# Interleaving the first block's work with the weight unpacking, and joining the attention's small products

## Chip, cores, metric

One core of a Trainium2 chip. The metric is the device time of one launch in microseconds (us): the median of three runs of the kernel before is 931.48 us (930.40 to 931.63).

## What is computed

Chunked attention (each of 36 chunks of 64 tokens attends to itself, per head), then two MLPs: a PReLU MLP of width 2048 and a bilinear MLP of width 1536. The model width is 512, there are 2304 tokens, and inputs and output are float32.

```python
scores = (1 / sqrt(64)) * q_c @ k_c.T          # per chunk of 64 tokens and head
attn = softmax(scores)                          # with 1e-9 added to the sum
x = (attn @ v_c)  -> (2304, 512)
h = x @ w_in;  g = max(h, 0) + alpha * min(h, 0);  x = g @ w_out
out = ((x @ w_a) * (x @ w_b)) @ w_o
```

## The kernel before

TensorE (PE) multiplies, VectorE (DVE) and ScalarE (ACT) do the elementwise work, and SyncE's queue (SP) issues all DMAs. The kernel works a float32 product out as three products of float32r parts: each operand is split into a rounded part hi (`to_hi`, L78, a copy on ACT) and the rest lo (`to_lo`, L81, a subtraction on DVE); `three` (L293) multiplies hi·hi, hi·lo and lo·hi.

The weights arrive as 64-bit values. A unit is a 128x512 tile of weights (`units`, L89); the first MLP has 32 of them, i0, i1, then i2, o0, i3, o1 and so on. `w_load` (L96) brings a unit of 512 KB into one of three staging buffers. `unpack_ops` (L107) makes float32 of it: on DVE two 16-bit operations (L122, L126) that write the two halves of wz, on ACT the widening (L125), on DVE the shift-and-or (L129). After that `split` makes hi and lo of the unit.

Tokens go in blocks of 512, 256, 512, 512 and 512, a group being 128 tokens. An opening, written out by hand as a list of steps (`order1`, L478), computes the attention of the first block's four groups and unpacks the first four units. Then the loop at L488 takes the blocks. For each of 16 slices j of the first MLP it runs `s1` (L307: 12 products to h), `prelu` (L310: neg and pos on ACT, pos on DVE, gh on ACT, gl on DVE) and, two iterations late, `s2` (L324: 12 products into four accumulator banks). In block 0 each iteration also splits the two units unpacked in the iteration before (L509), unpacks two more (L510) and starts two or three weight loads (L511), all ahead of `prelu` in program order. Engines run in program order, so this order is the order of the work on each engine.

The attention of the next block is laid between these as steps: `att_steps` (L398) lists them, and `advance` (L493) issues them spread evenly over two slots per iteration (in block 0 from slot 8 on). For one group these are: `att_T` (L204), eight 128x128 transposes of k and q and two copies on ACT; `att_S` (L216), 32 products of 64x64 into two banks; `att_M` (L230) on DVE: maximum and subtraction; `att_X` (L244), the exponential on ACT; `att_N` (L247), the sum and the division on DVE; `att_PT` (L256), four transposes of the probabilities and a copy (eT); `att_O` (L265), 32 products of 64x64 into two banks, whose hi and lo become the next block's x. A pool of four PSUM banks (`ps_p`, L66) is shared by h and all of the attention; it goes round in the order of the calls. The second MLP (L533) has no attention beside it, and the change does not touch it.

Of the kernel before, what the change touches and what calls it, by code (L numbers as in the profile page):

```python
# [8 lines left out]
F32 = mybir.dt.float32  # L9
# [9 lines left out]
def chunk_attention_prelu_mlp_bilinear_mlp(  # L19
# [55 lines left out]
    def wtile(name, dt=F32R):  # L75
        return wp.tile([P, DM], dt, tag="w", name=name)
# [7 lines left out]
    def split(*a):  # L84
        to_hi(*a)
        to_lo(*a)
# [17 lines left out]
                out=raw.rearrange("p (k f) -> p k f", k=KD), in_=src.rearrange("(k p) f -> p k f", p=P)  # L104
            )

    def unpack_ops(i):  # L107

        raw = raws.pop(i)
        hw = raw.rearrange("p (f t) -> p f t", t=2)[:, :, 1]
        if i < len(units) - 4:
            x = wtile("wx", I32)
        else:
            x = tp.tile([P, DM], I32, tag="t", name="wx")
        xs[i] = x
        z = wtile("wz", I32)
        z2 = z.bitcast(U16).rearrange("p (f t) -> p f t", t=2)  # L120
        h2 = raw.bitcast(U16).rearrange("p (f t) -> p f t", t=4)
        yield nc.vector.tensor_scalar(  # L122
            out=z2[:, :, 0], in0=h2[:, :, 1], scalar1=13, scalar2=None, op0=ALU.logical_shift_right
        )
        yield nc.scalar.activation(out=x.bitcast(F32), in_=hw.bitcast(F32), func=AF.Copy, scale=2.0 ** -112)  # L125
        yield nc.vector.tensor_scalar(  # L126
            out=z2[:, :, 1], in0=h2[:, :, 3], scalar1=1 << 15, scalar2=None, op0=ALU.bitwise_and
        )
        yield nc.vector.scalar_tensor_tensor(  # L129
            out=x, in0=x, scalar=3, in1=z, op0=ALU.logical_shift_left, op1=ALU.bitwise_or  # L130
        )

    def w_parts(i):
        m, j = units[i]
# [36 lines left out]
    def runs(t, n):  # L171
        done = 0
        while done < n:
# [2 lines left out]
            yield done, step, b, s  # L176
            done += step

    def load(nm, u):
        a = att[nm, u] = wtile(f"{nm}{u}", F32)  # L180
        for off, n, b, s in runs(u * P, P):
            nc.sync.dma_start(
                out=a[off:off + n].rearrange("p (h d) -> p h d", h=H),
                in_={"q": q, "k": k, "v": v}[nm][b, :, s:s + n, :].rearrange("h p d -> p h d"),
            )

    def load_qk(u):
        load("k", u)
        load("q", u)

    def load_v(u):
        load("v", u)
# [3 lines left out]
    def att_bank(u, nm):  # L196

        if u < sizes[0] // P:
            n_early[0] += 1
            if n_early[0] % 2:  # L200
                return acc_p.tile([P, DM], F32, tag="acc", name=nm)
        return bank(nm)

    def att_T(u, nms="kq"):  # L204
        for nm in nms:
            src = att.pop((nm, u))
            ps = att_bank(u, "psT")
            for g in range(KD):
                nc.tensor.transpose(ps[:, g * P:(g + 1) * P], src[:, g * P:(g + 1) * P], ident)  # L209
            t = att[nm + "T", u] = wtile(f"{nm}T{u}", F32)  # L210
            nc.scalar.activation(out=t, in_=ps, func=AF.Copy)  # L211

    def half(i):
        return slice(i * CH, (i + 1) * CH)

    def att_S(u):  # L216
        qT, kT = (att.pop((nm, u)).rearrange("p (g t) -> p g t", g=KD) for nm in ("qT", "kT"))
        pss = [att_bank(u, "psS") for _ in range(2)]
        for y in range(2):
            for c in range(2):  # L220
                for e in range(2):
                    for x in (e, 1 - e):
                        r, g, t = half(e), 2 * x + y, half(c)
                        nc.tensor.matmul(  # L224
                            out=pss[e][half(x), half(2 * y + c)], lhsT=qT[r, g, t], rhs=kT[r, g, t],
                            start=True, stop=True,
                        )
        att["s", u] = pss
# [33 lines left out]
        nc.scalar.activation(out=t, in_=ps, func=AF.Copy)  # L262
        att["eT", u] = t

    def att_O(u, xh, xl, col):  # L265
        eT, v_ = att.pop(("eT", u)), att.pop(("v", u))
        pss = [att_bank(u, "psO") for _ in range(2)]
        for g in range(KD):
            x, y = divmod(g, 2)
            for c in range(2):  # L270
                for e in (c, 1 - c):
                    nc.tensor.matmul(  # L272
                        out=pss[c][half(e), half(g)], lhsT=v_[half(c), half(2 * g + e)],
                        rhs=eT[half(c), half(4 * e + 2 * y + x)], start=True, stop=True,
                    )
        cols = [slice(col + c * CH, col + (c + 1) * CH) for c in range(2)]
        return [
            (xh[:, :, f], xl[:, :, f], ps[:, :KD * CH].rearrange("p (g i) -> p g i", g=KD))
            for f, ps in zip(cols, pss)
        ]  # L280

    def each(fn, parts):
        for part in parts:
            fn(*part)
# [22 lines left out]
    def s1(j, x, n):  # L307
        return proj(W["i", j], x, n)[:, :n]

    def prelu(j, h):  # L310
        n = h.shape[1]
        pos = tp.tile([P, NB], F32, tag="t", name="pos")[:, :n]
        neg = tp.tile([P, NB], F32, tag="t", name="neg")[:, :n]
        nc.scalar.activation(out=neg, in_=h, func=AF.Relu, scale=-1.0)  # L314
        nc.scalar.activation(out=pos, in_=h, func=AF.Relu)  # L315
        nc.vector.scalar_tensor_tensor(  # L316
            out=pos, in0=neg, scalar=nalpha_sb[:, j:j + 1], in1=pos, op0=ALU.mult, op1=ALU.add
        )
        gh = gp.tile([P, NB], F32R, tag="gh", name="gh")[:, :n]
        gl = gp.tile([P, NB], F32R, tag="gl", name="gl")[:, :n]  # L320
        split(gh, gl, pos)
        return gh, gl

    def s2(j, g, acc, n):  # L324
        wh, wl = W["o", j]
# [70 lines left out]
            pend.pop(0)()  # L396

    def att_steps(b, x):  # L398
        t0, n = blocks[b]
        steps = []  # L400

        def last(u):
            o = att_O(u, *x, u * P - t0)
            each(to_hi, o)
            each(to_lo, o)
            if u + 2 < NU:
                load_v(u + 2)

        def first(u):
            att_T(u)  # L410
            if u + 1 < NU:
                load_qk(u + 1)

        us = range(t0 // P, (t0 + n) // P)
        for w in range(len(us) + 2):
            T, A, Z = us[w:w + 1], us[max(w - 1, 0):w], us[max(w - 2, 0):max(w - 1, 0)]
            for u in T:
                steps.append(lambda u=u: first(u))
            for u in A:
                steps.append(lambda u=u: (att_X(u), weave(att_N(u))))  # L420
            for u in Z:
                steps.append(lambda u=u: att_PT(u))
            for u in T:
                steps.append(lambda u=u: (att_S(u), att_M(u)))
            for u in Z:
                steps.append(lambda u=u: last(u))
        return steps

    with tc.manual_schedule():
        n0 = sizes[0] // P  # L430
# [52 lines left out]
        for t in order1.split():  # L483
            early[t[0]](int(t[1:]))
        done["unpack"], done["split"] = 4, 3
        nc.scalar.mul(nalpha_sb, alpha_sb, -1.0)

        for b, (t0, n) in enumerate(blocks):  # L488
            nxt = xtiles("x")
            steps = att_steps(b + 1, nxt) if b + 1 < NBLK else []  # L490
            taken = [0]

            def advance(slot, first=8 if b == 0 else 0, last=2 * J1 - 3, steps=steps, taken=taken):  # L493
                want = -(-len(steps) * (slot + 1 - first) // (last + 1 - first))
                while taken[0] < min(want, len(steps)):
                    steps[taken[0]]()
                    taken[0] += 1

            for j in range(J1):
                if b == 0:  # L500
                    if j == 1:
                        load_qk(n0)
                    if j == 2:
                        load_v(n0)
                    if j == 3:
                        load_v(n0 + 1)
                h = h0[0][:, :n] if not (b or j) else s1(j, x, n)
                if b == 0:
                    w_split(min(2 * j + 4, NU1))  # L509
                    w_unpack(min(2 * j + 6, NU1))  # L510
                    w_dma(min(2 * j + 9, NU1))  # L511
                advance(2 * j)
                g = prelu(j, h)

                def second(b=b, j=j, g=g, n=n, nxt=nxt):
                    if j == 0:
                        acc[0] = new_acc()
                    s2(j, g, acc[0], n)
                    if j == J1 - 1:
                        end1(b, acc[0], n, nxt)  # L520

                pend.append(second)
                flush(2)
                advance(2 * j + 1)
                if b == NBLK - 1 and j >= 2:
                    ready = NU1 + 3 * (j - 2) // 2
                    w_dma(ready + 3)
                    w_unpack(ready + 1)
                    w_split(ready)
            x = nxt  # L530
# [60 lines left out]
```

## Time and profile before

| | |
|---|---|
| median of 3 runs | 931.48 us |
| profiled execution, its own time | 930.36 us |
| its span, first to last instruction | 928.6 us |
| PE busy | 904.1 us (97%) |
| DVE busy | 408.1 us (44%) |
| ACT busy | 337.1 us (36%) |
| DMA, mean over the span | 68 GB/s |

How to read it: a share is an average over stages. The opening lasts to some 31 us, block 0 to about 132, block 1 (256 tokens) to 193, blocks 2 and 3 to 389; then come the last block of the first MLP and the second MLP. In the timeline rows the columns are the start, the duration (a row of several instructions: from the first's start to the last's end), engine, line, operation, output and inputs, shape, count, and in brackets the idle time before and what ended it. Instructions on one engine overlap at their ends, so the pace of a stream is the distance between starts.

### The profile page before, as it was taken

What the parts mean: (1) busy time and instruction counts of PE and PEld (TensorE: products, weight loads), DVE (VectorE), ACT (ScalarE), POOL (GpSimd) and SP (SyncE); (2) the same over time, 40 slices, a digit from 0 to 9 for tenths busy, and PEclk for the clock granted to TensorE, in tenths of its full rate; (3) what the DMA queues carried; (4) which work ended last, traced back from release to release, by engine and by line L of the source; (5) the groups of instructions that cost most, each with busy time, mean ns of one, the idle gap of its engine ahead of it and who ended that gap; (6) DMA issues with size and microseconds to landing.
All of it is one profiled execution on the core that took longest, in us unless ns stands there. A gap on an engine that the chain in (4) does not pass through costs nothing.

```text
span 928.6 us, 13023 instructions
## 1 busy us (share of the span) xinstructions
PE 904.1 (97%) x5426; PEld 756.6 (81%) x5426; DVE 408.1 (44%) x762; ACT 337.1 (36%) x636; POOL 0.7 (0%) x6
## 2 busy tenths in 40 slices
PE   7889799999999999999999999999999999999998
PEld 5667689988888887888888888888888888888897
DVE  5888865543433443358865662211221122111212
ACT  5655655443343443345644442111121112111211
POOL 0000000000000000000000000000000000000000
PEclk9999999999999999999999999999999999999999
DMA  8665423221111300044433430200020002000100
GB/s 207 210 204 174 147 58 103 58 55 37 38 33 23 91 13 12 1 159 137 156 116 91 137 114 1 90 1 1 1 91 0 1 1 69 1 0 1 46 1 23
DMA packets 88810, 62.70 MB, mean 68 GB/s; under 512 B 59824, under 2 KB 81328, under 8 KB 88752
## 3 DMA queue, kind: packets, MB, share of 16 engines
q1 hardware_dynamic: 88752, 61.88, 22.5%
q8 instruction: 42, 0.69, 0.3%
q14 instruction: 16, 0.13, 0.1%
HBM read 53.49 MB, written 8.39 MB: 67 GB/s over the span
## 4 chain that ended last, share of the span: by engine, by line
PE 88%; DVE 9%; ACT 1%; issue 1%; DMA 0%; SPq 0%; DVEq 0%
PE psh L296 50%; PE acc L296 34%; DVE wx L129 2%; PE psT L209 1%; PE psO L272 1%; DVE wz L126 1%; DVE wz L122 1%; PE psS L224 1%; DVE pos L316 1%; ACT gh L79 1%; DVE gl L82 1%; PE psP L260 1%; DMA k<-in_k_dram 0%; DVE mx L237 0%; DVE e L239 0%
## 5 line engine op out<-in xcount | busy, mean ns | idle before, releaser
L335 DVE TENSOR_TENSOR b_sb<-psh,b_sb 128x512 f32<-128x512 f32 (+1 forms) x60 | 38.3, 638 | 272.9 <-PE psh L296 272.9
L316 DVE SCALAR_TENSOR_TENSOR pos<-neg,nalpha_sb,pos 128x512 f32<-128x512 f32 (+1 forms) x80 | 55.6, 695 | 95.4 <-ACT pos L315 95.2
L333 ACT ACTIVATE b_sb<-psh 128x512 f32<-128x512 f32 (+1 forms) x60 | 33.1, 552 | 167.9 <-PE psh L296 167.9
L79 ACT ACTIVATE ch<-b_sb 128x512 fp32r<-128x512 f32 (+1 forms) x60 | 35.3, 589 | 153.5 <-DVE b_sb L335 153.5
L79 ACT ACTIVATE gh<-pos 128x512 fp32r<-128x512 f32 (+1 forms) x80 | 47.1, 589 | 98.7 <-DVE pos L316 98.7
L82 DVE TENSOR_TENSOR gl<-pos,gh 128x512 fp32r<-128x512 f32 (+1 forms) x80 | 51.1, 638 | 52.4 <-ACT gh L79 52.4
L314 ACT ACTIVATE neg<-psh 128x512 f32<-128x512 f32 (+1 forms) x80 | 44.1, 551 | 75.0 <-PE psh L296 75.0
L82 DVE TENSOR_TENSOR cl<-b_sb,ch 128x512 fp32r<-128x512 f32 (+1 forms) x60 | 38.3, 639 | 39.3 <-ACT ch L79 39.3
L129 DVE SCALAR_TENSOR_TENSOR wx<-wx,wz 128x512 int32<-128x512 int32 x68 | 47.1, 692 | 8.0 <-ACT wx L125 0.8
L315 ACT ACTIVATE pos<-psh 128x512 f32<-128x512 f32 (+1 forms) x80 | 44.2, 553 | 0.0
L125 ACT ACTIVATE wx<-raw 128x512 f32<-128x512 f32 x68 | 42.4, 662 | 3.6 <-DMA raw<-in_moe_w_b_dram 2.9
L126 DVE TENSOR_SCALAR wz<-raw 128x512 uint16<-128x512 uint16 x68 | 30.8, 453 | 0.0
L122 DVE TENSOR_SCALAR wz<-raw 128x512 uint16<-128x512 uint16 x68 | 28.1, 458 | 2.1 <-DMA raw<-in_moe_w_b_dram 2.1
L237 DVE TENSOR_REDUCE mx<-psS 128x4 f32<-128x256 f32 x36 | 13.5, 417 | 19.5 <-PE psS L224 19.5
L262 ACT ACTIVATE eT<-psP 128x512 f32<-128x512 f32 x18 | 10.7, 597 | 23.8 <-PE psP L260 23.8
L272 PEld LDWEIGHTS psO<-eT,v 64*64 64x64 f32 x576 | 10.6, 139 | 10.4 <-ACT eT L262 6.5
L82 DVE TENSOR_TENSOR xl<-psO,xh 128x256 fp32r<-128x256 f32 x36 | 13.4, 417 | 11.9 <-ACT xh L79 11.7
L272 PE MATMUL psO<-eT,v 64*64 64x64 f32 x576 | 13.1, 229 | 5.6 <-ACT eT L262 5.6
L224 PEld LDWEIGHTS psS<-kT,qT 64*64 64x64 f32 x576 | 10.0, 134 | 8.1 <-ACT qT L211 4.2
L250 DVE TENSOR_REDUCE sm<-e 128x8 f32<-128x512 f32 x18 | 12.3, 682 | 8.3 <-ACT e L245 8.0
L211 ACT ACTIVATE kT<-psT 128x512 f32<-128x512 f32 x18 | 10.7, 595 | 13.8 <-PE psT L209 13.8
L79 ACT ACTIVATE xh<-psO 128x256 fp32r<-128x256 f32 x36 | 11.6, 382 | 11.3 <-PE psO L272 11.3
(721 smaller groups left out, 2530.3 us busy)
## 6 DMA issues: line engine op xcount, KB each, us to landing
raw<-in_moe_w_out_dram SPq DMA_DIRECT2D x28, 512.0 KB, 3.6
raw<-in_moe_w_in_dram SPq DMA_DIRECT2D x16, 512.0 KB, 5.0
raw<-in_moe_w_b_dram SPq DMA_DIRECT2D x12, 512.0 KB, 4.5
raw<-in_moe_w_a_dram SPq DMA_DIRECT2D x12, 512.0 KB, 3.5
k<-in_k_dram SPq DMA_DIRECT2D x16, 256.0 KB, 3.3
q<-in_q_dram SPq DMA_DIRECT2D x16, 256.0 KB, 3.7
v<-in_v_dram SPq DMA_DIRECT2D x16, 256.0 KB, 2.8
out_dram<-os SPq DMA_DIRECT2D x8, 512.0 KB, 2.8
```

Of the source, the lines that this page charges most:

```text
L79: nc.scalar.activation(out=hi, in_=src, func=AF.Copy)
L82: nc.vector.tensor_tensor(out=lo, in0=src, in1=hi.bitcast(F32), op=ALU.subtract)
L122: yield nc.vector.tensor_scalar(out=z2[:, :, 0], in0=h2[:, :, 1], scalar1=13, scalar2=None, op0=ALU.logical_shift_right)
L125: yield nc.scalar.activation(out=x.bitcast(F32), in_=hw.bitcast(F32), func=AF.Copy, scale=2.0 ** -112)
L126: yield nc.vector.tensor_scalar(out=z2[:, :, 1], in0=h2[:, :, 3], scalar1=1 << 15, scalar2=None, op0=ALU.bitwise_and)
L129: yield nc.vector.scalar_tensor_tensor(out=x, in0=x, scalar=3, in1=z, op0=ALU.logical_shift_left, op1=ALU.bitwise_or)
L296: nc.tensor.matmul(out=ps, lhsT=a, rhs=b, start=(i == 0 and first), stop=(i == n_i - 1 and a is wl))
L314: nc.scalar.activation(out=neg, in_=h, func=AF.Relu, scale=-1.0)
L315: nc.scalar.activation(out=pos, in_=h, func=AF.Relu)
L316: nc.vector.scalar_tensor_tensor(out=pos, in0=neg, scalar=nalpha_sb[:, j:j + 1], in1=pos, op0=ALU.mult, op1=ALU.add)
L333: nc.scalar.activation(out=b_sb, in_=pb, func=AF.Copy)
L335: nc.vector.tensor_tensor(out=b_sb, in0=pa, in1=b_sb, op=ALU.mult)
```

## The change

In block 0 `prelu` and the unpacking are cut into parts and issued interleaved, in an order written out (`prelu_unpacking`). The widening comes first in a unit's unpacking, and a unit's hi follows its shift-and-or at once, an iteration earlier than before. Attention steps return what they leave for later (`rest`), which is issued after `prelu` (`settle`). Block 0's steps have fixed slots, and both groups of that attention share the two score banks and the two output banks. In the later blocks a group's transposes stand with the transposes of the probabilities of the group before (`turn`), and its scores with the outputs of the group before, in the two halves of the same two banks (`multiply`). `att_TQ` replaces `att_T` there: k and q are transposed by 64x64 products with the identity, 32 for a group, and the two copies stay. The opening keeps `att_T`. The loads of q, k and v for block 0's attention move from iterations 1, 2 and 3 to 1, 3, 4 and 6.

```diff
     def unpack_ops(i, act_first=False):
...
+    def unpack_parts(i):
+        u = unpack_ops(i, True)
+        next(u)
+        yield
+        next(u), next(u)
+        yield
+        next(u)
+        wparts[i] = w_parts(i)
+        to_hi(*wparts[i])
+        yield
...
+    def att_TQ(u):
+        src = [att.pop((nm, u)) for nm in "kq"]
+        pss = [bank("psT") for _ in range(2)]
+        for i, a in enumerate(src):
+            for g in range(KD):
+                for c in range(2):
+                    for e in (c, 1 - c):
+                        nc.tensor.matmul(
+                            out=pss[c][half(e), half(i * KD + g)], lhsT=a[half(c), half(2 * g + e)],
+                            rhs=ident[half(c), half(c)], start=True, stop=True,
+                        )
+        ts = [wtile(f"kq{u}{c}", F32) for c in range(2)]
+        for t, ps in zip(ts, pss):
+            nc.scalar.activation(out=t, in_=ps, func=AF.Copy)
...
+    def prelu_unpacking(j, h, load, attend, settle):
+        g = []
+        act = prelu_parts(j, h, g)
+        next(act)
+        rest = attend()
+        new = [unpack_parts(i) for i in todo("unpack", min(2 * j + 6, NU1))]
+        old = [wparts.pop(i) for i in todo("split", min(2 * j + 4, NU1))]
+        for p in old:
+            to_lo(*p)
+        for c in new:
+            next(c)
+        for c in new[:1]:
+            next(c)
+        next(act)
+        next(act)
+        for c in new[1:]:
+            next(c)
+        load()
+        for c in new[:1]:
+            next(c)
+        next(act)
+        for c in new[1:]:
+            next(c)
+        settle(rest)
+        return g
...
     def att_steps(b, x):
...
+        def turn(w):
+            for u in us[w:w + 1]:
+                att_TQ(u)
+                if u + 1 < NU:
+                    load_qk(u + 1)
+            for u in us[max(w - 1, 0):w]:
+                att_PT(u)
+            return lambda: None
+
+        def multiply(w):
+            pss = [bank("psSO") for _ in range(2)]
+            now, before = us[w:w + 1], us[max(w - 1, 0):w]
+            for u in now:
+                att_S(u, [ps[:, :KD * CH] for ps in pss])
+            o = []
+            for u in before:
+                o += att_O(u, *x, u * P - t0, [ps[:, KD * CH:] for ps in pss])
+                if u + 2 < NU:
+                    load_v(u + 2)
+            each(to_hi, o)
+
+            def then():
+                for u in now:
+                    att_M(u)
+                each(to_lo, o)
+
+            return then
...
+        if b == 1:
+            u0, u1 = us
+            return [
+                (8, only(lambda: att_TQ(u0))),
+                (10, only(lambda: (att_TQ(u1), load_qk(u1 + 1)))),
+                (14, both_S),
+                (16, lambda: lambda: att_M(u1)),
+                (18, lambda: soften(u0)),
+                (20, lambda: soften(u1)),
+                (24, only(lambda: [att_PT(u) for u in us])),
+                (27, both_O),
+            ]
         steps = []
...
+        for w in range(len(us) + 1):
+            steps += [lambda w=w: turn(w), lambda w=w: multiply(w)]
+            steps += [lambda u=u: soften(u) for u in us[w:w + 1]]
+        last = 2 * J1 - 3
+        return [(-(-last * i // (len(steps) - 1)), s) for i, s in enumerate(steps)]
...
                 if b == 0:
-                    w_split(min(2 * j + 4, NU1))
-                    w_unpack(min(2 * j + 6, NU1))
-                    w_dma(min(2 * j + 9, NU1))
-                advance(2 * j)
-                g = prelu(j, h)
+                    g = prelu_unpacking(j, h, lambda: w_dma(min(2 * j + 9, NU1)), lambda: advance(2 * j), settle)
+                else:
+                    rest = advance(2 * j)
+                    g = prelu(j, h)
+                    settle(rest)
```

In `prelu_parts` the calls of `next` issue: neg and pos on ACT; pos on DVE; gh; gl. `soften(u)` issues `att_X` and leaves `att_N` for later; `both_S` and `both_O` do a product of both groups into one pair of banks.

## Rows read from the trace of the kernel before

**Rows 1.** Stretches by time: busy time of each engine, then clock, DMA share, GB/s.

```profile
20.00:120.00 100.00, 85.06 (x544) 68.02 (x536) 86.02 (x170) 59.66 (x117) 0.00 (x0) 0.97 0.59 178
120.00:389.00 269.00, 269.00 (x2149) 227.67 (x2148) 119.41 (x240) 116.11 (x241) 0.00 (x0) 1.00 0.17 43
```

**Rows 2.** Timeline of DVE, one iteration of block 0.

```profile
42.47 0.75 DVE L316 SCALAR_TENSOR_TENSOR pos<-neg,nalpha_sb,pos 128x512 f32<-128x512 f32 x1
43.91 0.69 DVE L82 TENSOR_TENSOR gl<-pos,gh 128x512 fp32r<-128x512 f32 x1 [0.70 <-ACT gh L79]
44.52 0.68 DVE L82 TENSOR_TENSOR wi4l<-wx,wi4h 128x512 fp32r<-128x512 f32 x1
...
45.73 0.81 DVE L122 TENSOR_SCALAR wz<-raw 128x512 uint16<-128x512 uint16 x2
46.42 0.45 DVE L126 TENSOR_SCALAR wz<-raw 128x512 uint16<-128x512 uint16 x1
46.98 0.69 DVE L129 SCALAR_TENSOR_TENSOR wx<-wx,wz 128x512 int32<-128x512 int32 x1
...
48.76 0.75 DVE L316 SCALAR_TENSOR_TENSOR pos<-neg,nalpha_sb,pos 128x512 f32<-128x512 f32 x1
```

**Rows 3.** Timeline of PE in blocks 2 and 3, around scores and around transposes.

```profile
252.51 0.39 PE L296 MATMUL acc<-gh,wo7l 128*128 128x512 f32 x1
252.83 0.69 PE L224 MATMUL psS<-kT,qT 64*64 64x64 f32 x32
...
253.79 0.39 PE L296 MATMUL psh<-xl,wi10h 128*128 128x512 f32 x1
...
289.78 0.39 PE L296 MATMUL psh<-xh,wi0h 128*128 128x512 f32 x1
...
292.27 0.39 PE L296 MATMUL psh<-xh,wi0l 128*128 128x512 f32 x1
292.51 0.60 PE L209 MATMUL psT<-ident,k 128*128 128x128 f32 x4
...
293.61 0.40 PE L296 MATMUL acc<-gl,wo14h 128*128 128x512 f32 x1
```

**Rows 4.** Waits of PE, 20 to 122 us: us in total, times, longest.

```profile
PE psO L272 <- ACT eT L262: 5.6, 2, 5.0
...
PE psT L209 <- DVE e L239: 1.2, 1, 1.2
```

**Rows 5.** Timeline of ACT, the same iteration as rows 2.

```profile
43.25 0.63 ACT L79 ACTIVATE gh<-pos 128x512 fp32r<-128x512 f32 x1 [2.48 <-DVE pos L316]
...
44.83 1.23 ACT L125 ACTIVATE wx<-raw 128x512 f32<-128x512 f32 x2
45.97 0.57 ACT L314 ACTIVATE neg<-psh 128x512 f32<-128x512 f32 x1
```

**Rows 6.** The staging tiles raw: time from a load's issue to its landing.

```profile
DMA to landing us min/median/max: 3.3/4.1/7.1
```

**Rows 7.** Timeline of DVE and PE: the opening's end, and two later products.

```profile
31.19 0.69 DVE L129 SCALAR_TENSOR_TENSOR wx<-wx,wz 128x512 int32<-128x512 int32 x1
...
39.16 0.63 PE L296 MATMUL acc<-gh,wo0h 128*128 128x512 f32 x1
...
132.49 0.28 PE L296 MATMUL psh<-xh,wi0h 128*128 128x256 f32 x1
```

**Rows 8.** The tile of the scores: its products, ns min/median/max, first and last start.

```profile
L224 PE MATMUL psS<-kT,qT x576: 218/218/267, 6.6 to 352.7; 64*64 64x64 f32 x192
```

**Rows 9.** Timeline of DVE: a softmax's sum and division, a maximum and subtraction, ends.

```profile
81.58 0.68 DVE L250 TENSOR_REDUCE sm<-e 128x8 f32<-128x512 f32 x1
...
83.35 0.74 DVE L316 SCALAR_TENSOR_TENSOR pos<-neg,nalpha_sb,pos 128x512 f32<-128x512 f32 x1
...
89.64 0.75 DVE L237 TENSOR_REDUCE mx<-psS 128x4 f32<-128x256 f32 x2
...
90.97 0.74 DVE L316 SCALAR_TENSOR_TENSOR pos<-neg,nalpha_sb,pos 128x512 f32<-128x512 f32 x1
```

More of the change, by code (lines that the diff above doesn't have):

```diff
@@ L105, in w_load, with unpack_ops @@
             )
-    def unpack_ops(i):
+    def unpack_ops(i, act_first=False):
         raw = raws.pop(i)
@@ L121, in unpack_ops, with widen @@
         h2 = raw.bitcast(U16).rearrange("p (f t) -> p f t", t=4)
+        def widen():
+            return nc.scalar.activation(out=x.bitcast(F32), in_=hw.bitcast(F32), func=AF.Copy, scale=2.0 ** -112)
+        if act_first:
+            yield widen()
         yield nc.vector.tensor_scalar(
@@ L124, in unpack_ops @@
         )
-        yield nc.scalar.activation(out=x.bitcast(F32), in_=hw.bitcast(F32), func=AF.Copy, scale=2.0 ** -112)
+        if not act_first:
+            yield widen()
         yield nc.vector.tensor_scalar(
@@ L131, in unpack_ops @@
         )
+    wparts = {}
+    def unpack_parts(i):
[8 more added lines that the diff above has]
+        yield
     def w_parts(i):
@@ L177, in runs, with half @@
             done += step
+    def half(i):
+        return slice(i * CH, (i + 1) * CH)
     def load(nm, u):
@@ L209, in att_T, with att_S @@
                 nc.tensor.transpose(ps[:, g * P:(g + 1) * P], src[:, g * P:(g + 1) * P], ident)
-            t = att[nm + "T", u] = wtile(f"{nm}T{u}", F32)
+            t = wtile(f"{nm}T{u}", F32)
             nc.scalar.activation(out=t, in_=ps, func=AF.Copy)
[L213 to L218, printed above, removed]
+            att[nm + "T", u] = lambda r, g, c, t=t: t[r, half(2 * g + c)]
+    def att_TQ(u):
[12 more added lines that the diff above has]
+            nc.scalar.activation(out=t, in_=ps, func=AF.Copy)
+        for i, nm in enumerate("kq"):
+            att[nm + "T", u] = lambda r, g, c, i=i: ts[c][r, half(i * KD + g)]
+    def att_S(u, pss=None):
+        qT, kT = att.pop(("qT", u)), att.pop(("kT", u))
+        pss = pss or [att_bank(u, "psS") for _ in range(2)]
         for y in range(2):
@@ L222, in att_S @@
                     for x in (e, 1 - e):
-                        r, g, t = half(e), 2 * x + y, half(c)
+                        i = half(e), 2 * x + y, c
                         nc.tensor.matmul(
-                            out=pss[e][half(x), half(2 * y + c)], lhsT=qT[r, g, t], rhs=kT[r, g, t],
+                            out=pss[e][half(x), half(2 * y + c)], lhsT=qT(*i), rhs=kT(*i),
                             start=True, stop=True,
@@ L263, in att_PT, with att_O @@
         att["eT", u] = t
-    def att_O(u, xh, xl, col):
+    def att_O(u, xh, xl, col, pss=None):
         eT, v_ = att.pop(("eT", u)), att.pop(("v", u))
-        pss = [att_bank(u, "psO") for _ in range(2)]
+        pss = pss or [att_bank(u, "psO") for _ in range(2)]
         for g in range(KD):
@@ L308, in s1, with prelu_parts @@
         return proj(W["i", j], x, n)[:, :n]
-    def prelu(j, h):
+    def prelu_parts(j, h, g):
         n = h.shape[1]
@@ L314, in prelu @@
         nc.scalar.activation(out=neg, in_=h, func=AF.Relu, scale=-1.0)
-        nc.scalar.activation(out=pos, in_=h, func=AF.Relu)
-        nc.vector.scalar_tensor_tensor(
+        yield nc.scalar.activation(out=pos, in_=h, func=AF.Relu)
+        yield nc.vector.scalar_tensor_tensor(
             out=pos, in0=neg, scalar=nalpha_sb[:, j:j + 1], in1=pos, op0=ALU.mult, op1=ALU.add
@@ L320, in prelu @@
         gl = gp.tile([P, NB], F32R, tag="gl", name="gl")[:, :n]
-        split(gh, gl, pos)
-        return gh, gl
+        g[:] = gh, gl
+        to_hi(gh, gl, pos)
+        yield
+        to_lo(gh, gl, pos)
+        yield
+    def prelu(j, h):
+        g = []
+        for _ in prelu_parts(j, h, g):
+            pass
+        return g
+    def prelu_unpacking(j, h, load, attend, settle):
+        g = []
+        act = prelu_parts(j, h, g)
[20 more added lines that the diff above has]
+        settle(rest)
+        return g
     def s2(j, g, acc, n):
@@ L399, in att_steps @@
         t0, n = blocks[b]
-        steps = []
[L402 to L426, printed above, removed]
@@ L427, in att_steps @@
-        return steps
+        us = range(t0 // P, (t0 + n) // P)
+        def turn(w):
[22 more added lines that the diff above has]
+            return then
@@ new lines, in soften, with both, both_S, both_O @@
+        def soften(u):
+            att_X(u)
+            return lambda: weave(att_N(u))
+        def both(product):
+            pss = [bank("psSO") for _ in range(2)]
+            return [product(u, [ps[:, i * KD * CH:(i + 1) * KD * CH] for ps in pss]) for i, u in enumerate(us)]
+        def both_S():
+            both(att_S)
+            return lambda: att_M(us[0])
+        def both_O():
+            o = sum(both(lambda u, pss: att_O(u, *x, u * P - t0, pss)), [])
+            each(to_hi, o)
+            for u in us:
+                load_v(u + 2)
+            return lambda: each(to_lo, o)
@@ new lines, in only @@
+        def only(fn):
+            return lambda: fn() and None or (lambda: None)
+        if b == 1:
[10 more added lines that the diff above has]
+            ]
@@ L485, in chunk_attention_prelu_mlp_bilinear_mlp @@
         done["unpack"], done["split"] = 4, 3
+        wparts[3] = w_parts(3)
+        to_hi(*wparts[3])
         nc.scalar.mul(nalpha_sb, alpha_sb, -1.0)
@@ L490, in chunk_attention_prelu_mlp_bilinear_mlp, with advance, settle @@
             steps = att_steps(b + 1, nxt) if b + 1 < NBLK else []
[L491 to L497, printed above, removed]
+            def advance(slot, steps=steps):
+                rest = []
+                while steps and steps[0][0] <= slot:
+                    rest.append(steps.pop(0)[1]())
+                return rest
+            def settle(rest):
+                for then in rest:
+                    then()
             for j in range(J1):
                 if b == 0:
[L501 to L506, printed above, removed]
+                    if j in (1, 3):
+                        load_qk(n0 + j // 2)
+                    if j in (4, 6):
+                        load_v(n0 + j // 2 - 2)
                 h = h0[0][:, :n] if not (b or j) else s1(j, x, n)
                 if b == 0:
-                    w_split(min(2 * j + 4, NU1))
-                    w_unpack(min(2 * j + 6, NU1))
-                    w_dma(min(2 * j + 9, NU1))
-                advance(2 * j)
-                g = prelu(j, h)
+                    g = prelu_unpacking(j, h, lambda: w_dma(min(2 * j + 9, NU1)), lambda: advance(2 * j), settle)
[3 more added lines that the diff above has]
+                    settle(rest)
                 def second(b=b, j=j, g=g, n=n, nxt=nxt):
@@ L523, in chunk_attention_prelu_mlp_bilinear_mlp @@
                 flush(2)
-                advance(2 * j + 1)
+                settle(advance(2 * j + 1))
                 if b == NBLK - 1 and j >= 2:
```

## The prediction

> **What bounds the kernel now.** I read the stages by time first. From 120 us on TensorE (PE) is busy without a gap; between 20 and 120 us it is idle for 14.9 of 100 us, and there VectorE (DVE) is busy 86.0 us [rows 1]. That stretch is the first block, in which each iteration also unpacks two weight tiles. Next I read DVE's order of time through one of its iterations [rows 2]: from one pos to the next 6.28 us pass. It holds a stall of 0.70 us, where gl waits for ScalarE's gh, and two places where an unpack step waits for the one just before it (0.56 us from the 16-bit operation to the shift-and-or, while two independent ones took 0.69 us together). PE's 24 products of an iteration take less: twelve starts lie (292.27 − 289.78)/11 = 0.2264 us apart [rows 3], so 24 take 5.43 us. So DVE, not PE, sets the pace here, and PE's waits follow from it, as the view of waits lists them [rows 4]: 5.6 us at outputs for eT's copy (one of 5.0), 1.2 us at transposes for a bank that the softmax still reads. PE cannot catch these up later: it is full to the end.
>
> **The first block's iteration.** The new order on DVE is: two lo; the two 16-bit operations of the first unit; pos; the two of the second; shift-and-or of the first; gl; shift-and-or of the second. Nothing is removed. At the paces of rows 2 it is 2 × 0.605 (lo) + 4 × 0.345 + 0.61 (pos) + 2 × 0.61 + 0.61 (gl) = 5.03 us. gl comes 1.9 us after pos starts, and gh is out 1.44 us after it (the row's gl), so that stall is hidden behind the second unit's work; if that cover were gone it would cost 0.83 us again. A new wait takes a little back: the second lo needs its hi, now issued at the end of the iteration before, 0.75 + 0.66 us after the shift-and-or starts, and DVE is there after 1.21: 0.2 us. So 5.23 us.
>
> The wait added is on ScalarE (ACT), which runs in order: neg and pos now stand ahead of the widening, and behind them stand widening, gh and both hi. From ACT's rows [rows 5] gh and two hi take 1.58 us, two widenings 1.14, neg and pos 0.97. The ring of the engines (last shift-and-or, its hi, neg, pos, two widenings, gh, gl, shift-and-or) is 0.1 + 0.53 + 0.97 + 1.14 + 0.66 + 0.61 + 0.61 = 4.6 us: shorter than 5.23, so it hides, except in iterations 4 and 5, where two copies of some 0.5 us stand in it: 0.4 us each.
>
> SyncE's queue: the weight loads move behind the first unit's second 16-bit operation, whose end frees their staging buffer; the block's q, k and v loads move one to three iterations later, ahead of them. From that point to the next iteration's second widening are some 5 us, and a load lands in 4.1 us (median, 7.1 at most) [rows 6]. I cost it at nothing; landing times above 5 us are the bound.
>
> **When PE is full.** The last shift-and-or of the opening starts at 31.19 [rows 7]. Its hi (31.94), lo (32.6), two 16-bit operations, then pos(0) at 33.9, and gl(0) out at 33.9 + 0.61 + 0.69 + 0.61 + 0.7 = 36.5 us. Before, PE was still in the first acc products at 39.16, behind a wait, and they were 0.63 us long at the lower level of the clock [rows 7], where rows 3 have 0.39. That loss goes with the wait or is taken up by the wait for banks below. From 36.3 us PE has until the next block's first product 13 × 12 + 14 × 12 = 324 products, 73.35 us, and the attention of two groups.
>
> A set of 32 64x64 products (scores) costs, from the last product before to the second one after, 253.79 − 252.51 − 2 × 0.226 = 0.83 us [rows 3]. The 32 themselves start (0.69 − 0.218)/31 = 0.015 us apart, 0.49 us in all (0.218 is one product's length [rows 8]); 0.34 us is paid around them. Eight transposes of q and k cost 293.61 − 292.27 − 0.45 = 0.89 us [rows 3]. The new transposes are 32 such products: I take 0.83. Scores of two groups in one go: 0.34 + 64 × 0.0152 = 1.31 instead of 1.65. So the block's attention takes 2 × 0.83 + 2 × 1.31 + two transposes of probabilities at half of 0.89 = 5.2 us. Gapless end: 36.3 + 73.35 + 5.2 = 114.9 us, against 132.49 [rows 7].
>
> Two waits remain. The banks go round in fours: the second transposes (wanted at 36.3 + 6 × 2.72 + 0.83 = 53.4) need the banks of h(4) and of the first transposes, which ACT empties behind iteration 3's last hi: pos(3) 49.6 + 2.5 + 0.75 + 0.53, then neg, pos and a copy: 55.0. Wait 1.6 us. Both groups' scores share two banks until the second maximum-and-subtract (1.33 us [rows 9]) ends iteration 8 on DVE, at 33.9 + 8 × 5.23 + 1.33 + 0.8 + 3.1 + 1.4 = 82.5, while s1 of iteration 10 wants one at 36.3 + 2.72 + 7 × 5.43 + 1.66 + 1.31 + 1.6 = 81.6: 0.9 us. End 117.4, **a gain of 15.1 us**. DVE stays ahead: gl(13) is out at 33.9 + 13 × 5.23 + 2 × 1.33 + 2 × 1.77 (softmax [rows 9]) + 1.7 + 2 = 111.8, and PE wants it at 114.7. Bounds: 17.6 us without either wait; 6.28 us again for each iteration gives nothing.
>
> **The three blocks after it.** Each has four groups. Transposes: 12 × (0.89 − 0.83) = 0.7 us. Scores of one group and outputs of the one before are joined three times a block: 9 × 0.34 = 3.1 us. Bounds: nothing from joining (0.34 may belong to each set), or all of it. The cost: transposes of probabilities now stand right behind those of the next group, two half-iterations after their softmax was begun; in the block of 256 tokens two are 2.9 us, and exponential (0.6), pos and gl there (0.9) and softmax (1.77) with hand-offs are over 3.3. I take 1.0 us for four such places, between 0 and 3. **Gain 2.8 us** (between −2.3 and 3.8).
>
> The Trainium skill, TensorEngine Tiling (Array Packing), Key Properties, says that changing the tiling mode drains TensorE; that speaks for the joining and against the new transposes, whose old form paid no such change, and the 0.34 us agrees. The Trainium skill, TensorE: Matmul & The Clock Gate, section "Wait — 56ns, not 53.3ns?", says that starts never come closer than about 25 ns; the scores' 15 ns differ from it, and the measurement decides. By that page the new transposes would take an estimated 1.14 us, and the sum would be 3.7 us less.
>
> Sum: 930.4 (this profiled run; its span is 928.6) − 15.1 − 2.8 = 912.5. The run lies 1.1 us under the median of 931.5, so the median comes to **913.6 us**.
>
> **Rivals.** (1) The ring, not PE, keeps the pace: if each 16-bit operation waits for its predecessor (0.56 instead of 0.345 for two or three of four), an iteration is 5.8 us; pos(13) is then at 117.2, and the block ends at 117.2 + 2 + 2.7 = 121.9, 4.5 us later: 918.1. For it: DVE is hardly slower than PE in my sum, only 0.2 us. Against: the 0.69 for two. Chance 0.20.
> (2) The 64x64 transposes run at half the pace of the scores (0.030 us apart, products waiting for each other): 0.34 + 0.97 = 1.31 us each, 12 × 0.48 = 5.8 us more: 919.4. Chance 0.08: rows 3 have the same products at 0.015. The floor in the Trainium skill, TensorE: Matmul & The Clock Gate, the section named above, lies between the two; both fall if the new trace shows 0.69 us for 32.
> (3) The change does not do what it says: the waits only move to banks, and the block keeps its pace: 931.5 − 2.8 = 928.7. Against: banks were waited for 1.2 us only [rows 4]. Chance 0.04.
> (4) Slower: weight loads arrive late. The second widening stands ahead of gh, and so of gl, the last shift-and-or and its hi; from widening to the point that issues the next load are some 4.4 us, and 0.4 us to issue. Two iterations then take 4.8 + landing: with 7.1 us 5.95, and from 7.8 us on an iteration is longer than before; at 9 us it is 6.9, 14 × 0.62 = 8.7 less 2.8: 937. Against: the median is 4.1, and this stage already moves 178 GB/s [rows 1]. Chance 0.03.
> The forecast has 0.62; the last 0.03 is more than I count (no waits and full joining), 910.
>
> **Numbers.** The forecast's own span is 910 to 918; the range 909 to 921 takes in rivals 1 and 2. About 0.2% can be told from no change. Faster 0.95, same 0.02, slower 0.03.
>
> **What would show it.** Right: gl no longer waits for gh between 36 and 112 us; pos to pos 5.2 to 5.5 us; the second block's first product near 117; 32 transposing products in 0.69 us, 64 joined in about 1.2; short PE waits at the second transposes and at h(10). Wrong: waits of widening for raw; 5.8 us a pace; PE idle over 2 us behind 120 us; transposes over 1 us.

## The result and the profile after

The changed kernel takes 916.36 us (median of 4 runs, 916.30 to 917.60), the kernel before 931.38 us: a ratio of 0.984, 95% interval 0.983 to 0.986. The forecast was 913.6 us (909 to 921). The profiled execution took 916.33 us, 14.0 us less than the one of before; its span is 914.6 us. PE is busy 902.4 us (99%), DVE 403.3 us, ACT 339.3 us. All medians and ratios here are over undisturbed runs; left out are two of the first seven runs of the last kernel below, gl right behind gh (1125.85 and 5144.81 us), and one run of the kernel before beside it (2319.62 us).

To see where the 14.0 us came from I take the start of each block's first product on PE. For block 1 and for the last block of the first MLP they stood at 132.49 [rows 7] and 389.19 us; blocks 2 and 3 began at 192.90 and 289.78 [rows 3]. The two of these that no row above shows, in the timeline of the kernel before:

```profile
192.90 0.40 PE L296 MATMUL psh<-xh,wi0h 128*128 128x512 f32 x1
...
389.19 0.39 PE L296 MATMUL psh<-xh,wi0h 128*128 128x512 f32 x1
```

In the timeline of the changed kernel the four are:

```profile
117.16 0.28 PE L335 MATMUL psh<-xh,wi0h 128*128 128x256 f32 x1
...
178.45 0.40 PE L335 MATMUL psh<-xh,wi0h 128*128 128x512 f32 x1
...
275.54 0.39 PE L335 MATMUL psh<-xh,wi0h 128*128 128x512 f32 x1
...
375.20 0.39 PE L335 MATMUL psh<-xh,wi0h 128*128 128x512 f32 x1
```

Up to block 1 the kernel gains 132.49 − 117.16 = 15.33 us. Over blocks 1 to 3 it **loses** 258.04 − 256.70 = 1.34 us: 0.88 in block 1, 0.21 and 0.25 in the next two. The rest of the kernel is as long as before. So the forecast's first term (15.1) held, and its second (a gain of 2.8) has the wrong sign.

The stretches by time (columns as in rows 1: bounds, length, then the busy time of PE, of PE's weight loads, of DVE, ACT and GpSimd):

```profile
20.00:110.00 90.00, 87.41 (x719) 71.67 (x720) 85.71 (x177) 66.05 (x123) 0.00 (x0) 0.99 0.68 200
...
120.00:389.00 269.00, 268.81 (x2721) 227.72 (x2721) 112.91 (x229) 111.36 (x230) 0.00 (x0) 1.00 0.17 41
```

DVE does in 90 us what it did in 100 [rows 1]: 85.7 us of work, now 95% busy, and PE is idle 2.6 us instead of 14.9. Behind 120 us PE is idle for only 0.19 us, so the loss there is work, not waiting. One iteration of block 0 on DVE, to set beside rows 2 (L355 is pos, L82 gl and the two lo):

```profile
39.41 0.74 DVE L355 SCALAR_TENSOR_TENSOR pos<-neg,nalpha_sb,pos 128x512 f32<-128x512 f32 x1
...
41.34 0.70 DVE L82 TENSOR_TENSOR gl<-pos,gh 128x512 fp32r<-128x512 f32 x1
...
42.55 0.70 DVE L82 TENSOR_TENSOR wi4l<-wx,wi4h 128x512 fp32r<-128x512 f32 x1
43.34 0.69 DVE L82 TENSOR_TENSOR wo2l<-wx,wo2h 128x512 fp32r<-128x512 f32 x1
...
44.64 0.74 DVE L355 SCALAR_TENSOR_TENSOR pos<-neg,nalpha_sb,pos 128x512 f32<-128x512 f32 x1
```

From pos to pos 5.23 us pass instead of 6.28, and gl carries no wait here. Only between the two lo is there 0.79 instead of 0.61 us: the second one's hi is late by 0.2 us. Up to 112 us three waits of gl are left, of 0.3 us each, in iterations 4, 5 and 12, where ACT also makes copies of the attention; in iterations 14 and 15, which have nothing left to unpack, gl waits 0.7 us again. DVE's waits from 36 to 112 us, then PE's from 30 to 117 us, to set beside rows 4 (each list is whole):

```profile
DVE gl L82 <- ACT gh L79: 0.9, 3, 0.3
```
```profile
PE acc L335 <- DVE gl L82: 0.5, 1, 0.5
PE psT L245 <- ACT pos L354: 0.2, 1, 0.2
PE psT L245 <- ACT kq L251: 0.2, 1, 0.2
```

The 5.0 us at the outputs are gone. Now the attention's sets in blocks 2 and 3 on PE: first a group's transposes alone, then scores and outputs joined.

```profile
278.04 0.39 PE L335 MATMUL psh<-xh,wi0l 128*128 128x512 f32 x1
278.35 0.69 PE L245 MATMUL psT<-ident,k 64*64 64x64 f32 x32
278.87 0.65 PE L245 MATMUL psT<-ident,q 64*64 64x64 f32 x32
...
279.78 0.39 PE L335 MATMUL acc<-gl,wo14h 128*128 128x512 f32 x1
...
306.40 0.39 PE L335 MATMUL acc<-gh,wo2l 128*128 128x512 f32 x1
306.72 0.69 PE L263 MATMUL psSO<-kq 64*64 64x64 f32 x32
307.24 0.65 PE L311 MATMUL psSO<-eT,v 64*64 64x64 f32 x32
...
308.15 0.39 PE L335 MATMUL psh<-xl,wi5h 128*128 128x512 f32 x1
```

By the same sum as for rows 3, the joined set costs 308.15 − 306.40 − 0.45 = 1.30 us, where I had 1.31. But the transposes cost 279.78 − 278.04 − 0.45 = 1.29 us, where I had 0.83: they are 64 rows, not 32. The code shows why. `att_S` calls the matmul 16 times for a group (2 × 2 × 2 × 2), and the trace has 32 rows for it (576 rows over 18 groups, [rows 8]): a float32 product of this form leaves two instructions on PE. `att_TQ` calls it 32 times, so there are 64. The old transposes leave one row for each call [rows 3]. (Where the kernel before is described, `att_S` has 32 products, which are its rows; where the change is, `att_TQ` has 32, which are its calls.)

### The profile page after: what moved, and what is told of

It is laid out like the page before. It is cut to its first block, busy times and chain, and to the rows that moved or that the text cites. A ratio compares the mean times of both kernels' runs of the same rounds, so it can differ in the third digit from the quotient of the medians.

```text
span 914.6 us, 14607 instructions
## 1 busy us (share of the span) xinstructions
PE 902.4 (99%) x6210; PEld 757.7 (83%) x6210; DVE 403.3 (44%) x762; ACT 339.3 (37%) x636; POOL 0.7 (0%) x6
## 4 chain that ended last, share of the span: by engine, by line
PE 94%; DVE 4%; ACT 1%; issue 0%; POOLq 0%; POOL 0%; DVEq 0%
PE psh L335 52%; PE acc L335 37%; PE psT L245 2%; PE psP L299 1%; PE psSO L263 1%; DVE wx L136 1%; PE psSO L311 1%; DVE wz L128 0%; DVE wz L133 0%; PE warm L570 0%; DVE xl L82 0%; DVE gl L82 0%; DVE e L278 0%; DVE mx L276 0%; DVE sm L289 0%
## 5 line engine op out<-in xcount | busy, mean ns | idle before, releaser
L355 DVE SCALAR_TENSOR_TENSOR pos<-neg,nalpha_sb,pos 128x512 f32<-128x512 f32 (+1 forms) x80 | 55.6, 695 | 120.8 <-ACT pos L354 120.7
L82 DVE TENSOR_TENSOR gl<-pos,gh 128x512 fp32r<-128x512 f32 (+1 forms) x80 | 51.0, 638 | 43.5 <-ACT gh L79 43.5
L82 DVE TENSOR_TENSOR cl<-b_sb,ch 128x512 fp32r<-128x512 f32 (+1 forms) x60 | 38.4, 639 | 39.3 <-ACT ch L79 39.3
L251 ACT ACTIVATE kq<-psT 128x512 f32<-128x512 f32 x28 | 15.2, 596 | 23.0 <-PE psT L245 22.9
L79 ACT ACTIVATE xh<-psSO 128x256 fp32r<-128x256 f32 x28 | 9.1, 381 | 16.3 <-PE psSO L311 16.3
L284 ACT ACTIVATE e<-e 128x512 f32<-128x512 f32 x18 | 11.2, 623 | 10.4 <-DVE e L278 10.4
L299 PE MATMUL psP<-ident,e 128*128 128x128 f32 x72 | 12.0, 294 | 2.4 <-ACT eT L301 1.7
L276 DVE TENSOR_REDUCE mx<-psSO 128x4 f32<-128x256 f32 x28 | 10.5, 417 | 5.2 <-ACT xh L79 5.2
L293 DVE TENSOR_TENSOR e<-e,rc 128x512 f32<-128x512 f32 x18 | 12.4, 691 | 0.6
L245 PEld LDWEIGHTS psT<-ident,k 64*64 64x64 f32 x448 | 8.0, 134 | 4.6 <-issue 1.8
L299 PEld LDWEIGHTS psP<-ident,e 128*128 128x128 f32 x72 | 8.3, 146 | 4.1 <-ACT eT L301 1.8
```

Of the source, the lines that this page charges most:

```text
L79: nc.scalar.activation(out=hi, in_=src, func=AF.Copy)
L82: nc.vector.tensor_tensor(out=lo, in0=src, in1=hi.bitcast(F32), op=ALU.subtract)
L355: yield nc.vector.scalar_tensor_tensor(out=pos, in0=neg, scalar=nalpha_sb[:, j:j + 1], in1=pos, op0=ALU.mult, op1=ALU.add)
```

## The experiments

Each run is the changed kernel with one part altered; each has runs of the kernel before beside it (medians 931.36 us, and 931.59 us for the doubled transposes and for gl right behind gh).

**The transposes.** `att_T` instead of `att_TQ` in all later blocks.

```diff
-                att_TQ(u)
+                att_T(u)
...
-                (8, only(lambda: att_TQ(u0))),
-                (10, only(lambda: (att_TQ(u1), load_qk(u1 + 1)))),
+                (8, only(lambda: att_T(u0))),
+                (10, only(lambda: (att_T(u1), load_qk(u1 + 1)))),
```

> The changed kernel, with k and q of the later blocks transposed by eight 128x128 transposes per group again. Theory (the 64x64 transposes are the term that was mis-sized: 64 rows per group on the matrix engine, 1.29 us, against 0.89 us): 12 x 0.40 = 4.8 us go in blocks 1 to 3 and up to 0.8 us in block 0, so about 911 us (910.5 to 912). Rival (the 64x64 form costs no more; what blocks 1 to 3 lost is waits behind the joined sets): 916 us or slower.

Measured: 912.76 us (912.37 to 913.17), ratio to before 0.980 (0.979 to 0.981). The rival falls. PE's timeline of one turn (transposes of k, q and of the probabilities), then the first products of block 1 and of the last block:

```profile
296.51 0.39 PE L335 MATMUL acc<-gh,wo1l 128*128 128x512 f32 x1
296.75 0.60 PE L232 MATMUL psT<-ident,k 128*128 128x128 f32 x4
...
298.29 0.40 PE L335 MATMUL psh<-xl,wi4h 128*128 128x512 f32 x1
...
117.03 0.28 PE L335 MATMUL psh<-xh,wi0h 128*128 128x256 f32 x1
...
371.43 0.39 PE L335 MATMUL psh<-xh,wi0h 128*128 128x512 f32 x1
```

A turn costs 298.29 − 296.51 − 0.45 = 1.33 us; in the changed kernel the same turn costs 1.69. Blocks 1 to 3 take 254.40 us, 3.64 less than with the 64x64 form and 2.30 less than before. Twelve groups at 0.36 to 0.40 would be some 4.5 us; two new waits of 0.3 us each at the probabilities' transposes give back 0.6. Block 0 gains only 0.13 us from its two: most of the 0.8 us that they save PE now waits, 0.3 us more at the second transposes, for a bank behind ACT's pos (0.62 instead of 0.33), and 0.36 us at the probabilities' transposes for DVE's softmax. So the theory holds with a smaller gain than expected (911 us), and this version is the fastest of all that ran.

**The joining.** In blocks 1 to 3, outputs one slot behind the scores, in banks of their own.

```diff
-            for u in before:
-                o += att_O(u, *x, u * P - t0, [ps[:, KD * CH:] for ps in pss])
...
+        def outputs(w):
+            u = us[w - 1]
+            o = att_O(u, *x, u * P - t0)
...
+        apart = [(steps[3 * w + 1][0] + 1, lambda w=w: outputs(w)) for w in range(1, len(us))]
```

> The changed kernel, with the outputs of blocks 1 to 3 one slot behind the scores and in banks of their own. Theory (0.34 us is paid once for each entry into 64x64 products): 9 x 0.35 = 3.2 us more, about 919.5 us. Rival (the 0.34 us belongs to each set, joined or not): 916.4 us within 0.5.

Measured: 921.75 us, ratio 0.990 (0.988 to 0.991), 5.4 us over the changed kernel. Its first products and its waits of PE from 117 to 390 us:

```profile
117.29 0.28 PE L335 MATMUL psh<-xh,wi0h 128*128 128x256 f32 x1
...
380.55 0.39 PE L335 MATMUL psh<-xh,wi0h 128*128 128x512 f32 x1
```
```profile
PE psh L335 <- DVE e L278: 1.1, 3, 0.5
PE psP L299 <- DVE e L293: 0.7, 1, 0.7
```

Blocks 1 to 3 are 263.26 − 258.04 = 5.22 us longer. Waits are 1.8 us of it, 3.4 remain: 0.38 us for each of the nine sets taken apart. The entry is paid again for each set that is taken apart, as expected; that PE then waits for DVE's softmax, at a bank and at the probabilities, was not expected.

**Doubling the transposes.** In blocks 1 to 3 each set of 64 is done twice in a row.

```diff
-        for i, a in enumerate(src):
+        for i, a in list(enumerate(src)) * (1 if u < (sizes[0] + sizes[1]) // P else 2):
```

> The changed kernel, with the 64x64 transposes of blocks 1 to 3 each done twice in a row into the same places. Theory (64 rows at 0.0152 us, the entry paid once, TensorE full so that all of it shows): 12 x 0.97 = 11.7 us more, 928.0 us. Rival (each set of 64 costs its 1.29 us however it is placed): 15.5 us more, 931.9 us. Third: transposes hidden beside other work: less than 8 us more.

Measured: 927.29 us, ratio 0.996 (0.994 to 0.997), 10.9 us over the changed kernel. One doubled set, and the last block's first product:

```profile
307.70 0.69 PE L245 MATMUL psT<-ident,k 64*64 64x64 f32 x32
308.21 0.65 PE L245 MATMUL psT<-ident,q 64*64 64x64 f32 x32
308.68 0.65 PE L245 MATMUL psT<-ident,k 64*64 64x64 f32 x32
...
386.13 0.39 PE L335 MATMUL psh<-xh,wi0h 128*128 128x512 f32 x1
```

386.13 − 375.20 is 10.93 us, or 0.91 for each set, where a set by itself costs 1.29: the 32 rows take 0.47 to 0.51 us from start to start here, and nothing is paid around a set that follows in the same form. The rival (each set its full price, 15.5 us) falls, and so does the third (less than 8): PE is full, and its extra work shows whole. The Trainium skill, TensorEngine Tiling (Array Packing), Key Properties, says that a change of the tiling mode drains TensorE. Both runs agree with it: 0.38 us more at each of nine further entries, nothing at repetitions.

**The old order in block 0, with the new attention.**

```diff
-        wparts[3] = w_parts(3)
-        to_hi(*wparts[3])
...
-                    g = prelu_unpacking(j, h, lambda: w_dma(min(2 * j + 9, NU1)), lambda: advance(2 * j), settle)
+                    w_split(min(2 * j + 4, NU1))
+                    w_unpack(min(2 * j + 6, NU1))
+                    w_dma(min(2 * j + 9, NU1))
```

> The changed kernel, with block 0's unpacking, splitting and PReLU in the order of before, and the new attention with its fixed slots. Theory (VectorE's pace of 6.28 us sets block 0): pos to pos 6.3 us again, the next block's first product at about 130 us, 928 to 930 us in all. Rival (the waits at the attention's steps were the loss, and the fixed slots took them away): within 3 us of 916.4, at most 919.5 us.

Measured: 930.39 us, ratio 0.999 (0.998 to 1.000). DVE's pos of two iterations, then block 1's first product:

```profile
42.82 0.74 DVE L355 SCALAR_TENSOR_TENSOR pos<-neg,nalpha_sb,pos 128x512 f32<-128x512 f32 x1
...
49.10 0.74 DVE L355 SCALAR_TENSOR_TENSOR pos<-neg,nalpha_sb,pos 128x512 f32<-128x512 f32 x1
...
130.60 0.28 PE L335 MATMUL psh<-xh,wi0h 128*128 128x256 f32 x1
```

6.28 us again, and 130.60: the new attention alone is worth 1.9 us in block 0. The rival falls. The waits at the outputs are gone here too, but PE waits elsewhere, 3.9 us at the probabilities' transposes for a bank that ACT's neg still reads and 2.2 us at the second transposes of q and k.

**The new order, with the old attention in block 0.**

```diff
-                (8, only(lambda: att_TQ(u0))),
...
-                (27, both_O),
+            return [(7 + -(-(22 * i + 1) // 10), only(s)) for i, s in enumerate(old)]
```

Here `old` lists the ten steps of before. With them the postponing (`rest`, `settle`) goes out of block 0's attention too: the softmax is issued right behind its exponential.

> The changed kernel, with block 0's attention as before: 128x128 transposes, single sets, ten steps spread over slots 8 to 27. Theory (the order sets VectorE's pace, but the old steps make TensorE wait for the copy of the probabilities in its program order): pos to pos 5.2 us outside the steps, one wait of 5 to 7 us at the first outputs, the next block's first product at about 125 us, 923 to 925 us in all. Rival (the order alone carries the whole gain of block 0): 916 to 917 us.

Measured: 926.22 us, ratio 0.994 (0.993 to 0.996). The timelines of PE and ACT (psP the transposes of the first group's probabilities, eT their copy, psO the outputs), and block 1's first product:

```profile
88.34 0.60 PE L299 MATMUL psP<-ident,e 128*128 128x128 f32 x4
...
100.10 0.58 ACT L301 ACTIVATE eT<-psP 128x512 f32<-128x512 f32 x1
...
100.73 1.13 PE L311 MATMUL psO<-eT,v 64*64 64x64 f32 x32 [6.30 <-ACT eT L301]
...
127.10 0.28 PE L335 MATMUL psh<-xh,wi0h 128*128 128x256 f32 x1
```

DVE's waits from 30 to 117 us, the largest:

```profile
DVE sm L289 <- ACT e L284: 3.4, 2, 2.2
```

The order alone is worth 132.49 − 127.10 = 5.4 us, and with the new attention 15.3: **the two parts are worth twice as much together (15.3) as the sum of each alone (5.4 + 1.9)**. PE transposes the probabilities at 88 us, but ACT, which is then almost two iterations further back in program order, copies them at 100 us; the outputs, two slots later in PE's order, hold PE for 6.3 us. In the changed kernel the outputs stand three slots behind, the copies follow the transposes by 6.7 us instead of 11.8, and no such wait is left. How much of this the slots do and how much the postponing is not shown, as this run takes both away: its DVE waits 3.4 us for the exponential, a wait that neither the kernel before nor the changed one has, and ACT falls back with it. I had expected the end at 125 us. Part of the difference is the clock: behind the wait the set is 1.13 us long instead of 0.69, and the granted clock is 0.50, the lower level of 1.2 GHz, from 100 to 106 us.

**gl right behind gh.** One call is moved ahead.

```diff
         next(act)
         next(act)
+        next(act)
         for c in new[1:]:
             next(c)
         load()
         for c in new[:1]:
             next(c)
-        next(act)
```

> The changed kernel, with gl of block 0 issued right behind gh, ahead of the second unit's 16-bit operations. Theory (the stall of gl behind gh is 0.83 us that the new order hides, and VectorE's 5.23 us leave only 0.2 us under TensorE's 5.43): pos to pos 6.0 to 6.1 us, block 0 ends 8 to 10 us later, 924 to 927 us in all. Rival (the gain came from splitting the weights an iteration earlier, the stall is hidden anyway by the lead of two iterations): 916 to 919 us.

Measured: 928.49 us (927.62 to 929.17), ratio 0.997 (0.996 to 0.998): more than the theory said, and the rival is out. A second look at the same kernel was for the trace.

> The same kernel as the run before with gl right behind gh, once more for a profile: its time is known (928.6 us), the question is where it goes. Theory: pos to pos 6.0 to 6.1 us on VectorE with a wait of gl for gh of 0.7 us in each iteration, and what is over 926 us lies in waits of TensorE at the attention's steps. Rival: the pace stays near 5.3 us and the time is lost behind block 0.

Measured: 928.43 us. DVE's timeline, PE's two longest waits from 30 to 390 us, and two stretches (the column before the DMA share is PE's clock):

```profile
40.33 0.74 DVE L355 SCALAR_TENSOR_TENSOR pos<-neg,nalpha_sb,pos 128x512 f32<-128x512 f32 x1
41.77 0.69 DVE L82 TENSOR_TENSOR gl<-pos,gh 128x512 fp32r<-128x512 f32 x1 [0.70 <-ACT gh L79]
...
46.34 0.74 DVE L355 SCALAR_TENSOR_TENSOR pos<-neg,nalpha_sb,pos 128x512 f32<-128x512 f32 x1
```
```profile
PE psP L299 <- DVE e L293: 4.0, 1, 4.0
PE psT L245 <- ACT pos L354: 3.0, 1, 3.0
```
```profile
100.00:105.00 5.00, 1.82 (x11) 1.28 (x9) 4.21 (x10) 2.26 (x5) 0.00 (x0) 0.88 0.53 155
105.00:110.00 5.00, 4.15 (x12) 3.50 (x13) 4.29 (x9) 2.33 (x5) 0.00 (x0) 0.50 0.36 110
```

The pace is 6.01 us, as the theory had it, with the stall of 0.70 us back. PE then waits 7.0 us at two attention steps. What I had left out is the clock: behind the one of 4.0 us the granted clock was 0.50, which is the lower level of 1.2 GHz, for the whole of 105 to 110 us. So one position in a list of calls carries 12.1 us of the median.

## Why the prediction was right, and where it was wrong

**DVE's pace: right.** 5.03 us by rows and 0.2 us for the late hi made 5.23; the trace has 5.21 to 5.23 in the iterations without attention. In iterations 4 and 5, where ACT makes the transposes' copies, I added 0.4 us; the trace has 5.6 us there, and in iteration 12 too, where the copies of the probabilities stand. Moving gl alone brought 6.01, and 5.23 with the 0.83 us of the prediction is 6.06.

**The end of block 0: right, with terms that cancel.** 117.4 foretold, 117.16 measured. The two waits of 1.6 and 0.9 us came to 0.3 us (0.18 and 0.15 in the timeline) and nothing. PE reached the first at 54.6 us and not at 53.4: its first transposes are 0.46 us longer, and the opening ended 0.3 us later than before (its last shift-and-or starts at 31.50, not 31.19); the rest of the 1.2 us is not taken apart. So the number owes something to luck: transposes that cost too much filled the time in which PE was to wait. (The sum to 82.5 us in the second wait makes 82.4.)

**"PE's waits follow from it": wrong in part.** I put the whole of PE's waiting down to DVE's pace, and of the waits of before I left out the one at the scores, 3.15 us for ACT's copy of q (its row is shown at the end). The order alone leaves 6.3 us of waiting at the outputs; the issue of the attention had to change too. The forecast summed the whole change, so the number did not suffer.

**The step that failed: "The new transposes are 32 such products: I take 0.83."** They are 32 calls and 64 rows. I read the scores' 32 rows as 32 calls without counting the loops. With 1.29 the term is 12 × (1.29 − 0.89) = 4.8 us lost instead of 0.7 gained. The gain of 2.8 less these 5.5, and without 0.8 us of waits that I had added and that are not there, is a loss of 1.9 us; measured are 1.34. The 0.6 us between lie in two smaller terms. A joined set saves 2 × 0.83 − 1.30 = 0.36 us, not 0.34. And transposes of probabilities that stand in a turn are cheaper, which I had not counted. By themselves they cost 225.35 − 224.45 − 0.45 = 0.45 us in the kernel before; a turn of the changed kernel costs 201.73 − 199.59 − 0.45 = 1.69, which is 0.40 more than its 64x64 transposes. The rows of before, then those of the changed kernel:

```profile
224.45 0.39 PE L296 MATMUL psh<-xh,wi5l 128*128 128x512 f32 x1
224.68 0.60 PE L260 MATMUL psP<-ident,e 128*128 128x128 f32 x4
...
225.35 0.40 PE L296 MATMUL acc<-gl,wo3h 128*128 128x512 f32 x1
```
```profile
199.59 0.39 PE L335 MATMUL acc<-gh,wo1l 128*128 128x512 f32 x1
...
201.73 0.39 PE L335 MATMUL psh<-xl,wi4h 128*128 128x512 f32 x1
```

With the prices of blocks 2 and 3 for all twelve groups the loss is 4.8 − 9 × 0.36 − 9 × 0.05 + 0.19 (idle) = 1.3 us. Why most of it, 0.88 us, lies in block 1 stays open. One of the prediction's own signs of being wrong, transposes over 1 us, came true.

Rival (2) had the price (1.31) and the wrong mechanism: the pace is that of the scores, 0.69 us for 32 rows, and there are twice as many. I had given it a chance of 0.08. That the blocks' loss of 1.3 us still lies within the bounds of their term (−2.3 to 3.8) is luck: those bounds were drawn for a joining that gives nothing and for up to 3 us of waits, and neither came. The starts of 15 ns also stand against the floor of about 25 ns that the Trainium skill, TensorE: Matmul & The Clock Gate, section "Wait — 56ns, not 53.3ns?", gives; the measurement decides.

**Joining: right.** 1.30 us for a joined set against 1.31, and taking them apart costs 0.38 us a set besides new waits. **Waits behind the joined turns: wrong.** 1.0 us foretold; PE's idle time over blocks 1 to 3 is 0.19 us.

Rivals 1, 3 and 4 fall: the pace is not 5.8 us, the waits did not move to banks, and no widening of block 0 waits for a load in the waits of ACT from 30 to 122 us.

## To carry to other kernels

Count a step's instructions from the loops and the rows together: how many rows one call leaves is part of the price, and in these traces a transpose done as a plain float32 product leaves two where the transposing form leaves one. A wait between two engines that work in program order can be hidden by issuing independent work between its ends, as the 0.70 us of gl are here, and a few positions decide it. An order that speeds up the bounding engine pays in full only if what the other engines wait for in program order moves with it; here either half alone gave less than half of the gain.

## What was not expected

A wait of PE can cost more than its length. In the kernel with gl early the waits of 3.0 and 4.0 us are followed by products at the lower clock (0.63 instead of 0.39 us for a product of 512 columns, the granted clock at 0.50 from 105 to 110 us). But the length of the wait alone does not decide it in these traces. In the kernel before, 1.8 us of waiting ahead of the first acc products is followed by products of 0.63 us [rows 7], while the 3.15 us at the scores is not: the 32 products behind it take the usual 0.69 us, and the granted clock is 1.00 from 60 to 64 us.

```profile
60.46 0.69 PE L224 MATMUL psS<-kT,qT 64*64 64x64 f32 x32 [3.15 <-ACT qT L211]
```

And the order and the placement of the attention are far from adding up: 5.4 and 1.9 us alone, 15.3 us together.
